# Maxima moved out of the first step of an attention kernel: a lead of 16 visits, two value units and six banks of maxima each

## The chip, the cores and the metric

The kernel runs on one core of a Trainium2 chip. The metric is the device time of one execution in microseconds (us); lower is better. The engines named below are PE (TensorE, matmuls), PEld (its weight loads, which overlap its matmuls), DVE (VectorE), ACT (ScalarE), POOL (GpSimd) and SP (SyncE, here only a queue for DMAs). L341 is line 341 of the kernel before.

## What is computed

Two attentions over the same x (2048 rows, 576 columns, 32 heads of 18), mixed by a gate for each row:

```python
g = _sigmoid((x * gate_w).sum(-1, keepdims=True))
a = _A_ref(x, A_wqkv, A_wo)           # 32 heads, each with its own keys and values
b = _B_ref(x, B_wq, B_wk, B_wv, B_wo) # 32 query heads, one shared key and value head
return g * a + (1 - g) * b
```

Each of the two is softmax(q k / sqrt(18)) v for every head, then a product with wo, in float32. The softmax is taken with the row maximum subtracted.

## The kernel before

**Stages.** The kernel treats the 64 heads alike and calls them u = 0 to 63; the first 32 share one key head. Stage one projects x to queries and keys (project, L147) and writes them to memory in DRAM as a high and a low part. The lead follows: it projects the values (project_v, L187) and computes the first row maxima (step_max, L341 and L350). Then comes the long loop over steps T = 0 to 1023, 16 steps to a head, taken in pairs; then the last output projections.

**A step.** A head has 2048 queries and 2048 keys. For the maxima, step (u, i) takes 128 queries against all keys: four banks of PSUM, each one matmul of 54 rows by 512 columns (pm, L341) and one reduction on DVE (mx, L350). For one step in each pair of the loop there is a shorter way: an extra "x" bank with a difference of keys goes through ACT (xb, L344) and is added by DVE to bank 0 on the fly (L347), so that bank 1 isn't needed. For the scores, step (u, i) takes 128 keys against all queries: four matmuls (ps, L376) and four exponentials on ACT (pt, L383). The values then multiply the exponentials (acc, L390), a step or two behind the scores. The operands lie twice in SBUF, from partition 0 and from partition 64; the argument low of step_max picks the copy at 0. A bank on the one and a bank on the other use different rows of the PE array.

**Maxima run ahead.** The scores of a head need the maxima of all its queries, so the maxima run LEAD = 22 steps ahead of the scores. After the 16 steps of a head, max_rows (L356, L358) reduces the four columns, transposes, splits the result on POOL and sends it by way of DRAM into the two extra rows of the query tile (m_d, then qs).

**The order** is written out by hand: each engine executes in the order in which the loop emits, and an engine waits only where data or a buffer is missing. Strings give the order inside a pair of steps: s a score bank, m and M maxima banks (M from the low copy), A and B the first and second step of the pair, P, h and H the values' matmuls, x the extra bank, V a number of value units.

```python
FIRST = "sA0 mA2 sA1 mA0 sA2 mA3 mA1 sA3 mB0 sB0 mB1 sB1 mB2 sB2 mB3 sB3 x"
PLAIN = "sA0 mA2 sA1 mA0 sA2 mA3 P sA3 mB0 sB0 mB1 sB1 mB2 h sB2 mB3 sB3 x H"
LEADS = "V.A mA0 MA1 mA2 MA3 V.B mB0 MB1 mB2 MB3"
```

The lead is the same loop with T from -22 to -2 and the string LEADS: 11 pairs of steps, so 22 groups of four maxima banks with one or two value units ahead of each, 32 units in all. Step T = 0 uses FIRST: the scores of steps 0 and 1 together with all eight maxima banks of steps 22 and 23. From T = 2 on it is PLAIN.

**Buffers.** Three rings of PSUM banks: ps_s (3 banks, for score banks and for the projections and value units), ps_m (4 banks, for maxima) and ps_o (1, acc). A tile takes the next bank of its ring and waits until the bank's last reader is done: ACT for scores and value units, DVE for maxima. A value unit is 14 matmuls of 288 columns, one copy by ACT into one of three staging tiles (vst, L190) and one DMA from ACT's queue to DRAM (v_d).

**Side work.** Between the steps of the lead, a generator (gates, L272 to L276) takes one step in each pair: it computes the gates with two small ACT operations, one on POOL and one on DVE, and some DMAs from SP. open_ph2 frees the buffers of stage one and opens those of the loop.

Of the kernel before, what the change touches and what calls it, by code (L numbers as in the profile page):

```python
# [8 lines left out]
F32 = mybir.dt.float32  # L9
# [12 lines left out]
NU = 2 * H  # L22
# [5 lines left out]
LEAD = 22  # L28
# [14 lines left out]
def gated_mix_kernel(ctx: ExitStack, tc: tile.TileContext, xT, wall, wv, wo, out):  # L43
    nc = tc.nc
    P = 128

    def dma(o, i, eng=None):
        o, i = (x.bitcast(F32) if x.dtype == F32R else x for x in (o, i))
        return (eng or nc.sync).dma_start(o, i)  # L49
# [3 lines left out]
    ps_s = ctx.enter_context(tc.tile_pool(name="ps_s", bufs=3, space=PSUM))  # L53
    ps_m = ctx.enter_context(tc.tile_pool(name="ps_m", bufs=4, space=PSUM))
# [57 lines left out]
    def split(src, h, l, eng_h, eng_l):  # L112
        if eng_h is nc.scalar:
            nc.scalar.activation(h, src, AF.Copy)
        else:
            eng_h.tensor_copy(h, src)  # L116
        if l is not None:
            eng_l.tensor_tensor(l, src, h.bitcast(F32), op=OP.subtract)
# [65 lines left out]
    def project_v(st_, hf, w):  # L184
        fp = ps_s.tile([P, 512], F32, name="ps")
        for n, (a, b, k, kr) in enumerate(PROJ):
            nc.tensor.matmul(fp[:, 0:288], X[b][:kr, k, st_ * P:(st_ + 1) * P], w[a][:kr, k, :],  # L187
                             start=(n == 0), stop=(n == len(PROJ) - 1))
        t = vst[st_ % 3]
        nc.scalar.activation(t[:, :, 0:18], fp[:, 0:288].rearrange("p (h d) -> p h d", d=18), AF.Copy)  # L190
        dma(v_d[st_, :, 304 * hf:304 * hf + 304], t.rearrange("p h d -> p (h d)"), nc.scalar)
# [5 lines left out]
    WV = []  # L197
# [70 lines left out]
    def gates():  # L268
        z = small.tile([P, 16], F32, name="z")
        dma(z, z_d.rearrange("(p f) -> p f", p=P))  # L270
        yield
        nc.scalar.activation(g2[:, 0, :], z, AF.Exp, scale=1.0)  # L272
        nc.scalar.activation(g2[:, 1, :], z, AF.Exp, scale=-1.0)
        nc.gpsimd.tensor_scalar(g2, g2, 1.0, None, op0=OP.add)
        yield
        nc.vector.reciprocal(g2, g2)  # L276
        yield
        for i in range(2):
            dma(g_d[i].rearrange("(p f) -> p f", p=P), g2[:, i, :])
        yield  # L280
        for i in range(2):
            dma(gu_d[H * i:H * i + H, :], g_d[i:i + 1, :].to_broadcast([H, S]))
# [15 lines left out]
    def open_ph2():  # L298
        ph1.close()
        L["pt"] = ctx.enter_context(tc.tile_pool(name="ppool", bufs=12, side="left"))  # L300
        L["work"] = ctx.enter_context(tc.tile_pool(name="work", bufs=2, side="left"))
        p2 = ctx.enter_context(tc.tile_pool(name="p2", bufs=1, side="right"))
        L["pool"] = p2
        L["ks"] = [p2.tile([P, S], F32R, name=f"ksa{i}") for i in range(2)] + [ksb]
        L["kds"] = [p2.tile([P, 512], F32R, name="kda"), kdb]
        L["oacc"] = p2.tile([P, 16, D], F32, name="oacc")
        for t in L["ks"][:2]:
            for b in (SB, MB):
                dma(t[b + 54:b + 56, :], ones_r)
# [8 lines left out]
    def kst(u):  # L318
        return ksb if u < H else L["ks"][(u - H) % 3]
# [6 lines left out]

    MX = {}

    def step_max(u, i, c, low=False):

        if u not in MX:
            MX[u] = mxs[u] if u < 2 else mxs[2 + u % 3]
        b = SB if low else MB
        if c == "x":
            k = L["kd", u if u >= H else 0][b:b + 54, :]
        else:
            k = kst(u)[b:b + 54, c * 512:(c + 1) * 512]
        pm = ps_m.tile([P, 512], F32, name="pm")  # L340
        nc.tensor.matmul(pm, qs[u % 3][b:b + 54, i * P:(i + 1) * P], k, start=True, stop=True)  # L341
        if c == "x":
            MX["x", u, i] = lead.tile([P, 512], F32, name="xb", bufs=2)
            nc.scalar.activation(MX["x", u, i], pm, AF.Relu)  # L344
        elif c == 0 and ("x", u, i) in MX:
            junk = lead.tile([P, 512], BF16, name="junk", bufs=1)
            nc.vector.tensor_tensor_reduce(junk, pm, MX.pop(("x", u, i)), 1.0, -3e38, op0=OP.add, op1=OP.max,  # L347
                                           accum_out=MX[u][:, i, c:c + 1])
        else:
            nc.vector.tensor_reduce(MX[u][:, i, c:c + 1], pm, axis=AX.X, op=OP.max)  # L350

    def max_rows(u):


        m = ms[u % 2]
        nc.vector.tensor_reduce(m[:, 0:16], MX.pop(u), axis=AX.X, op=OP.max, negate=True)  # L356
        mt = lead.tile([P, 32], F32, name="mt")
        nc.vector.transpose(mt, m)  # L358
        mh = lead.tile([P, 2, 32], F32R, name="mh")
        split(mt, mh[:, 0, :], mh[:, 1, :], nc.gpsimd, nc.gpsimd)  # L360
        md = m_d[u % 4]
        dma(md, mh.rearrange("p a f -> p (a f)"))
        for b in (SB, MB) if u > NU - 3 else (SB,):
            for a in range(2):
                dma(qs[u % 3][b + 54 + a:b + 55 + a, :].rearrange("o (i b f) -> o i b f", b=4, f=32),
                    md.rearrange("(b i) (o a f) -> o a i b f", i=32, o=1, a=2)[:, a, 0:16])
# [19 lines left out]
    def step_pv(u, i, a, b):  # L386


        for j in range(4):
            nc.tensor.matmul(acc[32 * j:32 * j + 19, a:b], v_of(u, i), PT[u, i, j][:, a:b],  # L390
                             start=(i == 0), stop=(i == 15), skip_group_check=True)
        if b == 512:
            for j in range(4):
                del PT[u, i, j]
# [170 lines left out]
    NSTEP = 16 * NU  # L565
    todo = []

    def pull(n):
        while n > 0 and todo:
            try:  # L570
                next(todo[0])
                n -= 1
            except StopIteration:
                todo.pop(0)
# [19 lines left out]
    slow = [gates()]  # L594
# [9 lines left out]
    def due(T, t0, t1, n):  # L604
        return (n * (T - t0 + 1)) // (t1 - t0) - (n * (T - t0)) // (t1 - t0) if t0 <= T < t1 else 0

    vunits = [(st_, hf) for hf in range(2) for st_ in range(16)]

    FIRST = "sA0 mA2 sA1 mA0 sA2 mA3 mA1 sA3 mB0 sB0 mB1 sB1 mB2 sB2 mB3 sB3 x"
    PLAIN = "sA0 mA2 sA1 mA0 sA2 mA3 P sA3 mB0 sB0 mB1 sB1 mB2 h sB2 mB3 sB3 x H"
    UNIT = "sA0 mA2 sA1 mA0 sA2 mA3 P sA3 mB0 sB0 mB1 sB1 mB2 U sB2 mB3 sB3 x Q"
    ALONE = "sA0 sA1 P U sA2 sA3 U sB0 sB1 h U sB2 sB3 H U"
    LEADS = "V.A mA0 MA1 mA2 MA3 V.B mB0 MB1 mB2 MB3"
    for T in range(-LEAD, NSTEP + 2, 2):
        if T == 0:
            open_ph2()
        for f in at.get(T, []) + at.get(T + 1, []):
            f()  # L620
        M = T + LEAD
        if M >= 16 and M % 16 == 0 and M // 16 - 1 < NU:
            max_rows(M // 16 - 1)
        alone = M >= NSTEP
        units = sum(due(t, Tb, Tc, 32) for t in (T, T + 1) for _, _, _, Tb, Tc in SEG)
        for op in (LEADS if T < 0 else FIRST if T == 0 else ALONE if alone else UNIT if units else PLAIN).split():
            k, second, c = op[0], op[1:2] == "B", op[2:]
            if k == "V":
                while len(vunits) > 32 * (-T - 1 - (c == "B")) // LEAD:
                    project_v(*vunits[0], WV[vunits[0][1]])  # L630
                    vunits.pop(0)
            elif k == "x":
                if M + 2 < NSTEP:
                    step_max(*divmod(M + 2, 16), "x")
            elif k in "mM":
                step_max(*divmod(M + second, 16), int(c), k == "M")
            elif k == "s":
                if T < NSTEP:
                    step_scores(*divmod(T + second, 16), int(c), alone)
            elif k == "U":  # L640
                pull(min(units, 1))
                units -= min(units, 1)
            elif T >= 2:
                step_pv(*divmod(T - (2 if k == "P" else 1), 16), 256 * (k == "H"), 256 if k == "h" else 512)
                if k in "HQ" and T % 16 == 0 and T < NSTEP:
                    head_out(T // 16 - 1)
        pull(units)
        if slow and M % 16:
            for _ in range(2 if T > 1000 else 1):
                if slow:  # L650
                    try:
                        next(slow[0])
                    except StopIteration:
                        slow.pop(0)
# [40 lines left out]
```

## Time and profile before

| | us |
|---|---|
| median of 3 runs | 2796.87 |
| lowest and highest | 2795.1, 2798.84 |
| the profiled execution | 2797.98 |
| its span in the profile | 2795.9 |
| PE busy in the span | 2767.0 |
| DVE busy | 2431.6 |
| ACT busy | 2430.6 |

The span is the time from the first to the last recorded instruction; the execution's own time is 2.1 us longer. Busy times are sums over an engine's instructions. A matmul's end is modelled, so PE looks busy while it in fact waits in line; the idle time of PEld, with what ended it, tells more about waits. The lead lies from 207.1 to 286.4 us of the span, the first step of the loop behind it. In rows of the timeline the columns are start, length, engine, line, operation, written and read tile, count, and in brackets the idle time ahead of it with what ended it.

### The profile page before, as it was taken

The page shows a single profiled execution, that of the slowest core. Times are in us where ns is not written, and L with a number is a line of the kernel's source. Part 1 is how long each engine was busy: PE and PEld are TensorE (multiplying, and loading weights), DVE is VectorE, ACT ScalarE, POOL GpSimd, SP SyncE. Part 2 cuts the span into 40 slices and gives each one's busy share as a digit, 9 for nine tenths or more (in the row PEclk, how much of TensorE's full clock was granted, in tenths as well). Part 3 has the DMA queues.
Part 4 walks back from the last instruction along what each step waited for, and adds up shares of the span by engine and source line. Part 5 has one row for each costly group of instructions (what it writes and reads, how often), then busy time and mean ns, then how long its engine had stood idle before and what let it go on. Part 6 is the DMA issues. An engine that isn't in the chain of part 4 may idle for free.

```text
span 2795.9 us, 57640 instructions
## 1 busy us (share of the span) xinstructions
PE 2767.0 (99%) x22140; PEld 1229.2 (44%) x22140; DVE 2431.6 (87%) x4524; ACT 2430.6 (87%) x4768; POOL 207.2 (7%) x364
## 2 busy tenths in 40 slices
PE   7999999999999999999999999999999999999999
PEld 5888433333333333333333444444444443334544
DVE  3346999999999999999999999899898999998865
ACT  3231899999999999999999999999999999998775
POOL 2220000001001000100110001000100011001000
PEclk9999999999999999999999999999999999999999
DMA  8662011111112111211143223232232323233412
GB/s 258 221 230 76 27 33 33 31 47 51 40 26 57 55 32 32 64 47 26 45 101 106 70 74 104 61 85 76 80 84 76 79 71 84 63 95 107 103 36 92
DMA packets 137143, 215.09 MB, mean 77 GB/s; under 512 B 55437, under 2 KB 94301, under 8 KB 125182
## 3 DMA queue, kind: packets, MB, share of 16 engines
q1 hardware_dynamic: 116156, 168.13, 22.6%
q10 hardware_dynamic: 14120, 22.30, 2.2%
q0 software_dynamic: 6592, 20.99, 2.2%
q8 instruction: 174, 2.85, 0.4%
q14 instruction: 101, 0.83, 0.1%
HBM read 137.31 MB, written 64.77 MB: 72 GB/s over the span
## 4 chain that ended last, share of the span: by engine, by line
PE 94%; DMA 3%; DVE 2%; issue 0%; SPq 0%; ACT 0%; POOL 0%; DVEq 0%; ACTq 0%; POOLq 0%
PE ps L376 40%; PE acc L390 38%; PE ps L147 5%; PE pm L341 5%; PE pm L506 4%; PE ps L187 2%; DVE mx L350 1%; DMA xs<-xT 1%; DVE oacc L560 0%; DMA qkl<-pl 0%; SPq L49 0%; DMA ksb<-qkl 0%; DMA qs<-qkh 0%; DMA ksa<-qkh 0%; DVE oacc L514 0%
## 5 line engine op out<-in xcount | busy, mean ns | idle before, releaser
L383 ACT ACTIVATE pt<-ps 128x512 f32<-128x512 f32 x4052 | 2128.6, 612 | 108.2 <-PE pm L341 45.6
L350 DVE TENSOR_REDUCE mx<-pm 128x1 f32<-128x512 f32 x3096 | 1975.9, 683 | 168.0 <-PE pm L341 126.7
L376 PE MATMUL ps<-qs,ksb 56*128 56x512 f32 x2688 | 908.2, 437 | 0.0
L341 PE MATMUL pm<-ksb,qs 54*128 54x512 f32 x2364 | 825.5, 446 | 1.1 <-DVE mx L350 0.3
L376 PEld LDWEIGHTS ps<-qs,ksb 56*128 56x128 f32 x2688 | 437.0, 184 | 685.2 <-ACT pt L383 665.1
L390 PE MATMUL acc<-pt,vb 128*19 128x256 f32 (+1 forms) x6144 | 592.5, 457 | 0.1
L390 PE MATMUL acc<-pt,vg 128*19 128x256 f32 (+1 forms) x5656 | 579.3, 481 | 0.7 <-DVE oe L400 0.4
L376 PE MATMUL ps<-qs,ksa 56*128 56x512 f32 x1364 | 455.7, 437 | 0.0
L341 PE MATMUL pm<-ksa,qs 54*128 54x512 f32 x1232 | 433.5, 443 | 0.0
L341 PEld LDWEIGHTS pm<-ksb,qs 54*128 54x128 f32 x2364 | 379.5, 184 | 10.6 <-DVE mx L350 4.1
L376 PEld LDWEIGHTS ps<-qs,ksa 56*128 56x128 f32 x1364 | 218.2, 184 | 342.9 <-ACT pt L383 316.8
L347 DVE CUSTOM_DVE_ANT_0 junk<-pm,xb 128x512 bf16<-128x512 f32 x500 | 339.9, 680 | 0.0
L344 ACT ACTIVATE xb<-pm 128x512 f32<-128x512 f32 x500 | 305.1, 610 | 0.0
L341 PEld LDWEIGHTS pm<-ksa,qs 54*128 54x128 f32 x1232 | 200.3, 184 | 0.9
L390 PEld LDWEIGHTS acc<-pt,vb 128*19 128x19 f32 x6144 | 104.2, 97 | 209.9 <-issue 199.9
L390 PEld LDWEIGHTS acc<-pt,vg 128*19 128x19 f32 x5656 | 95.9, 97 | 209.0 <-issue 197.7
L341 PE MATMUL pm<-kdb,qs 54*128 54x512 f32 x372 | 148.6, 400 | 0.0
L116 POOL CAST mh<-mt 128x32 fp32r<-128x32 f32 x64 | 13.4, 209 | 1683.4 <-DVE mt L358 1683.4
L156 DVE TENSOR_TENSOR pl<-ps,ph 128x512 fp32r<-128x512 f32 x56 | 38.4, 690 | 98.1 <-ACT ph L150 70.2
L150 ACT ACTIVATE ph<-ps 128x512 fp32r<-128x512 f32 x56 | 33.4, 597 | 102.4 <-PE ps L147 87.4
L147 PE MATMUL ps<-xh,wh 128*128 128x512 f32 x280 | 75.6, 401 | 20.9 <-ACT xh L210 13.4
L147 PE MATMUL ps<-xh,wl 128*128 128x512 f32 x280 | 73.5, 393 | 0.0
(99 smaller groups left out, 1334.7 us busy)
## 6 DMA issues: line engine op xcount, KB each, us to landing
qs<-qkh SPq DMA_DIRECT2D x244, 144.0 KB
qs<-qkl SPq DMA_DIRECT2D x122, 144.0 KB
qkh<-ph ACTq DMA_DIRECT2D x56, 256.0 KB
qkl<-pl POOLq DMA_DIRECT2D x56, 256.0 KB, 3.1
ksa<-qkh SPq DMA_DIRECT2D x88, 144.0 KB
onh<-oh SPq DMA_DIRECT2D x32, 256.0 KB
onl<-ol SPq DMA_DIRECT2D x32, 256.0 KB
oih<-onh SPq DMA_DIRECT2D x16, 512.0 KB
```

The lines of the kernel that those rows point to most:

```text
L147: nc.tensor.matmul(fp, w[a][:kr, k, :], X[b][:kr, k, cs], start=(n == 0), stop=(n == len(PROJ) - 1))
L150: nc.scalar.activation(h, fp, AF.Copy)
L156: nc.vector.tensor_tensor(l, fp, h.bitcast(F32), op=OP.subtract)
L187: nc.tensor.matmul(fp[:, 0:288], X[b][:kr, k, st_ * P:(st_ + 1) * P], w[a][:kr, k, :], start=(n == 0), stop=(n == len(PROJ) - 1))
L341: nc.tensor.matmul(pm, qs[u % 3][b:b + 54, i * P:(i + 1) * P], k, start=True, stop=True)
L344: nc.scalar.activation(MX["x", u, i], pm, AF.Relu)
L347: nc.vector.tensor_tensor_reduce(junk, pm, MX.pop(("x", u, i)), 1.0, -3e38, op0=OP.add, op1=OP.max, accum_out=MX[u][:, i, c:c + 1])
L350: nc.vector.tensor_reduce(MX[u][:, i, c:c + 1], pm, axis=AX.X, op=OP.max)
L376: nc.tensor.matmul(ps, kst(u)[b:b + 56, i * P:(i + 1) * P], qs[u % 3][b:b + 56, c * 512:(c + 1) * 512], start=True, stop=True)
L383: nc.scalar.activation(pt, ps, AF.Exp, scale=SCALE)
L390: nc.tensor.matmul(acc[32 * j:32 * j + 19, a:b], v_of(u, i), PT[u, i, j][:, a:b], start=(i == 0), stop=(i == 15), skip_group_check=True)
L506: nc.tensor.matmul(fp[:, 0:288], o[b][:r, t, s2 * P:(s2 + 1) * P], w[a][:r, t, 288 * hf:288 * hf + 288], start=(n == 0), stop=(n == 3 * nt ...
```

## The change

The lead becomes a loop of its own with 16 visits. Each visit emits two value units, then six maxima banks; 16 x 6 = 96 banks are the steps 0 to 23, two steps more than before. Odd banks use the low copy, as before. Of the six banks, the first two take their PSUM bank from the ring of the scores (ps_s), the other four from ps_m. max_rows of head 0 is emitted at the start of visit 11; before, it was emitted at T = -6, with three of the eleven pairs left. The gate generator takes its steps from visit 4 on. open_ph2 comes after the loop, as before right ahead of T = 0. FIRST, the string of step T = 0, keeps the scores and the x bank and loses its eight maxima banks. The steps from T = 2 on, LEAD and all buffers stay as they are.

```diff
--- before.py
+++ after.py
@@ -326,7 +326,7 @@
     MX = {}
-    def step_max(u, i, c, low=False):
+    def step_max(u, i, c, low=False, pool=ps_m):
@@ -337,7 +337,7 @@
             k = L["kd", u if u >= H else 0][b:b + 54, :]
         else:
             k = kst(u)[b:b + 54, c * 512:(c + 1) * 512]
-        pm = ps_m.tile([P, 512], F32, name="pm")
+        pm = pool.tile([P, 512], F32, name="pm" if pool is ps_m else "ps")
         nc.tensor.matmul(pm, qs[u % 3][b:b + 54, i * P:(i + 1) * P], k, start=True, stop=True)
         if c == "x":
             MX["x", u, i] = lead.tile([P, 512], F32, name="xb", bufs=2)
@@ -604,36 +604,45 @@
     def due(T, t0, t1, n):
         return (n * (T - t0 + 1)) // (t1 - t0) - (n * (T - t0)) // (t1 - t0) if t0 <= T < t1 else 0
     vunits = [(st_, hf) for hf in range(2) for st_ in range(16)]
-    FIRST = "sA0 mA2 sA1 mA0 sA2 mA3 mA1 sA3 mB0 sB0 mB1 sB1 mB2 sB2 mB3 sB3 x"
+    banks = [(M, c) for M in range(LEAD + 2) for c in range(4)]
+    for v in range(16):
+        if v == 11:
+            max_rows(0)
+        for st_, hf in vunits[2 * v:2 * v + 2]:
+            project_v(st_, hf, WV[hf])
+        for n, (M, c) in enumerate(banks[6 * v:6 * v + 6]):
+            step_max(*divmod(M, 16), c, c % 2 == 1, ps_s if n < 2 else ps_m)
+        if v >= 4 and slow:
+            try:
+                next(slow[0])
+            except StopIteration:
+                slow.pop(0)
+    open_ph2()
+    FIRST = "sA0 sA1 sA2 sA3 sB0 sB1 sB2 sB3 x"
     PLAIN = "sA0 mA2 sA1 mA0 sA2 mA3 P sA3 mB0 sB0 mB1 sB1 mB2 h sB2 mB3 sB3 x H"
     UNIT = "sA0 mA2 sA1 mA0 sA2 mA3 P sA3 mB0 sB0 mB1 sB1 mB2 U sB2 mB3 sB3 x Q"
     ALONE = "sA0 sA1 P U sA2 sA3 U sB0 sB1 h U sB2 sB3 H U"
-    LEADS = "V.A mA0 MA1 mA2 MA3 V.B mB0 MB1 mB2 MB3"
-    for T in range(-LEAD, NSTEP + 2, 2):
-        if T == 0:
-            open_ph2()
+    for T in range(0, NSTEP + 2, 2):
         for f in at.get(T, []) + at.get(T + 1, []):
             f()
         M = T + LEAD
-        if M >= 16 and M % 16 == 0 and M // 16 - 1 < NU:
+        if M % 16 == 0 and M // 16 - 1 < NU:
             max_rows(M // 16 - 1)
         alone = M >= NSTEP
         units = sum(due(t, Tb, Tc, 32) for t in (T, T + 1) for _, _, _, Tb, Tc in SEG)
-        for op in (LEADS if T < 0 else FIRST if T == 0 else ALONE if alone else UNIT if units else PLAIN).split():
+        for op in (FIRST if T == 0 else ALONE if alone else UNIT if units else PLAIN).split():
             k, second, c = op[0], op[1:2] == "B", op[2:]
-            if k == "V":
-                while len(vunits) > 32 * (-T - 1 - (c == "B")) // LEAD:
-                    project_v(*vunits[0], WV[vunits[0][1]])
-                    vunits.pop(0)
-            elif k == "x":
+            if k == "x":
                 if M + 2 < NSTEP:
                     step_max(*divmod(M + 2, 16), "x")
-            elif k in "mM":
-                step_max(*divmod(M + second, 16), int(c), k == "M")
+            elif k == "m":
+                step_max(*divmod(M + second, 16), int(c))
             elif k == "s":
                 if T < NSTEP:
                     step_scores(*divmod(T + second, 16), int(c), alone)
```

## The prediction

> **What bounds the kernel now.** I read the page's totals and its chain of work first, then the stages by windows, then the timeline of the two stages that the change touches.
>
> ```profile
> PE 2767.0 (99%) x22140; PEld 1229.2 (44%) x22140; DVE 2431.6 (87%) x4524; ACT 2430.6 (87%) x4768; POOL 207.2 (7%) x364
> ...
> PE 94%; DMA 3%; DVE 2%; issue 0%; SPq 0%; ACT 0%; POOL 0%; DVEq 0%; ACTq 0%; POOLq 0%
> ```
> ```profile
> 285.99:302.00 16.01, 14.93 (x76) 5.54 (x75) 13.37 (x25) 11.56 (x22) 0.00 (x0) 0.79 0.05 15
> 302.00:600.00 298.00, 297.99 (x2578) 113.08 (x2574) 286.14 (x539) 292.09 (x579) 3.69 (x16) 1.00 0.12 31
> ```
> The columns of the windows are length, busy time of PE, PEld, DVE, ACT and POOL, granted clock, DMA share. PE looks full everywhere, but its ends are modelled. In the long loop ACT is busy for 292.09 of 298.00 us, so the loop runs at ACT's pace. The 16 us before it are the odd ones out: ACT at 11.56, clock 0.79. The diff touches only the lead ahead of that stretch and its first step, so I treat everything behind it as shifted.
>
> The lead, from the chain in order of time and from the timeline:
>
> ```profile
> 219.31 2.06 PE ps L187 x14
> 221.37 0.78 PE pm L341 x3
> 222.15 3.88 PE ps L187 x28
> 226.04 0.66 PE pm L341 x2
> ```
> ```profile
> 207.10 0.81 PEld L187 LDWEIGHTS ps<-vwh,xh 128*128 128x128 f32 x5
> ...
> 222.08 0.69 PEld L187 LDWEIGHTS ps<-vwh,xh 128*128 128x128 f32 x5 [0.25 <-ACT vst L190]
> ...
> 225.97 0.73 PE L341 MATMUL pm<-ksb,qs 54*128 54x512 f32 x4
> 226.07 0.41 ACT L190 ACTIVATE vst<-ps 128x288 f32<-128x288 f32 x1 [1.43 <-PE ps L187]
> 226.51 2.48 DVE L350 TENSOR_REDUCE mx<-pm 128x1 f32<-128x512 f32 x4 [2.19 <-PE pm L341]
> ```
> PE sets the pace: two value units back to back take 3.88, four banks after them 0.66; a single unit takes 2.06, and the four banks after it 0.78, because DVE is still draining the previous four (2.48, 0.62 a bank). DVE then waits 2.19.
>
> The first step:
>
> ```profile
> 285.99 0.44 PEld L341 LDWEIGHTS pm<-ksb,qs 54*128 54x128 f32 x4 [0.17 <-issue]
> 286.36 0.19 PEld L376 LDWEIGHTS ps<-qs,ksb 56*128 56x128 f32 x1
> 286.53 7.86 DVE L350 TENSOR_REDUCE mx<-pm 128x1 f32<-128x512 f32 x13 [0.33 <-PE pm L341]
> 287.01 0.60 ACT L383 ACTIVATE pt<-ps 128x512 f32<-128x512 f32 x1 [0.50 <-PE ps L376]
> 287.27 0.18 PEld L341 LDWEIGHTS pm<-ksb,qs 54*128 54x128 f32 x1 [0.73 <-DVE mx L350]
> 287.27 0.50 PE L341 MATMUL pm<-ksb,qs 54*128 54x512 f32 x1 [0.30 <-DVE mx L350]
> 287.85 1.19 ACT L383 ACTIVATE pt<-ps 128x512 f32<-128x512 f32 x2 [0.24 <-PE pm L341]
> 287.87 0.18 PEld L341 LDWEIGHTS pm<-ksb,qs 54*128 54x128 f32 x1 [0.41 <-DVE mx L350]
> 292.88 0.60 ACT L344 ACTIVATE xb<-pm 128x512 f32<-128x512 f32 x1
> 294.68 1.91 PE L390 MATMUL acc<-pt,vb 128*19 128x512 f32 x8
> 296.52 0.28 PEld L376 LDWEIGHTS ps<-qs,ksb 56*128 56x128 f32 x1 [1.68 <-issue]
> 297.35 1.57 ACT L383 ACTIVATE pt<-ps 128x512 f32<-128x512 f32 x3 [2.36 <-PE pm L341]
> 300.26 0.60 ACT L344 ACTIVATE xb<-pm 128x512 f32<-128x512 f32 x1
> 301.35 1.05 PE L390 MATMUL acc<-pt,vb 128*19 128x512 f32 x8
> ```
> DVE bounds it: 13 reductions without a gap, and every score stands on PE behind a bank that waits for DVE (0.73, then 0.41, every 0.60 us). Then the values' matmuls of the second pair run at half speed, 1.91 against 1.05, and ACT idles 2.36.
>
> Where the loop has settled:
>
> ```profile
> 305.31 0.61 ACT L344 ACTIVATE xb<-pm 128x512 f32<-128x512 f32 x1
> 305.78 4.27 ACT L383 ACTIVATE pt<-ps 128x512 f32<-128x512 f32 x8
> 309.94 0.61 ACT L344 ACTIVATE xb<-pm 128x512 f32<-128x512 f32 x1
> ```
> Nine ACT operations from one x bank to the next, 309.94 - 305.31 = 4.63, or 0.514 each. My clock for the whole change is therefore when the x bank of the third pair (T = 4) reaches ACT: 305.31 now.
>
> **The change, part by part.** *The lead.* Before, it runs from 207.10 to the first score's weights at 286.36: 79.26 us for 32 value units and 88 banks in 22 groups. After, 16 visits hold the same units and 96 banks. A visit is 3.88 for the pair plus six banks. Two pairs of banks take 0.73 in their matmul row, one matmul 0.50 (the 287.27 row), so a further pair adds 0.23; if nothing overlapped it would be half of 0.66, 0.33, and at nothing the visit would be 0.23 less. I take 0.23: six banks 0.89, a visit 4.77, 16 visits 76.3. The last group is cut short as now: its score starts 0.37 after the group, not 0.66, so 0.3 less. The first score comes at 207.10 + 76.0 = 283.1, **3.2 us earlier** (between 1.6, with 0.33, and 6.9, with the third pair free). Eight more banks cost less than six group changes and the waits on DVE.
>
> What hides the rest: a visit's six reductions are 6 x 0.62 = 3.72 on DVE, under 4.77. The two banks in the scores' ring of three: a value unit's slot was last held by the second unit of the visit before (or, for the second unit, by its first bank). That unit's eviction ends at 226.48, 4.40 after its pair began at 222.08; the next pair starts at 4.77. So 0.37 us of cover; without it each visit is late by what is missing.
>
> *Moved steps.* Maxima of head 0 go out after visit 10, their DVE work at about 207.10 + 10 x 4.77 + 8.1 = 262.9.
>
> ```profile
> 268.72 0.22 DVE L356 TENSOR_REDUCE m<-mx 128x16 f32<-128x64 f32 x1
> ```
> ```profile
> 272.40 1.23 SPq L49 DMA_DIRECT2D qs<-m_d  x2
> ```
> From there to the end of the last DMA's issue is now 273.63 - 268.72 = 4.9; then 267.8, 15 us ahead of the first score at 283.1 (12.7 now). The gate steps run in visits 4 to 8, in ACT's idle 1.4 us; their DMAs stay on SP ahead of those of the maxima, three visits apart, and nothing else is on SP there. At nothing. The unit 16 uses the staging tile that unit 15 has just filled:
>
> ```profile
> 246.84 0.33 ACTq L49 DMA_DIRECT2D v_d<-vst  x1
> 249.12 0.41 ACT L190 ACTIVATE vst<-ps 128x288 f32<-128x288 f32 x1 [2.31 <-PE ps L187]
> ```
> That is 2.28 us now, with the wait on PE and not on the DMA; after, about 2.5. At nothing.
>
> *The first step.* Eight scores, an x bank, and no maxima, so ACT's 0.514 bounds it where DVE's 0.60 did. The first exponential follows its score by 287.01 - 286.36 = 0.65: 283.75. The second and third scores wait for slots of the last visit's two banks on DVE: 0.74 and 1.34 after DVE's start, as in the rows at 287.27 and 287.87, some 0.2 late in all. The x bank of the first step reaches ACT at 283.95 + 8 x 0.514 = 288.1 (now 292.88), that of the third pair, undisturbed, 9.26 later at 297.3: **8.0 us earlier** than 305.31.
>
> *The clock.* What may be late next is the array's clock:
>
> ```profile
> 286.40:291.50 5.10, 4.11 (x20) 1.49 (x17) 4.97 (x9) 3.75 (x8) 0.00 (x0) 1.00 0.13 43
> 291.50:291.56 0.06, 0.06 (x2) 0.06 (x2) 0.06 (x1) 0.06 (x1) 0.00 (x0) 0.94 0.00 0
> ...
> 291.60:298.35 6.75, 6.67 (x27) 2.31 (x31) 5.03 (x10) 4.13 (x9) 0.00 (x0) 0.50 0.01 2
> 298.45:302.00 3.55, 3.55 (x34) 1.23 (x26) 2.96 (x7) 3.18 (x7) 0.00 (x0) 1.00 0.00 0
> ```
> It fell at 291.55, 5.2 us after the dense lead ended, and came back at 298.37, 3.7 after dense work began again at 294.68. The new first step gives PE nine matmuls in 4.6 us, thinner than the 20 in 5.1. With the same delays: fall at 288.3, the values' matmuls of the second pair at about 288.9, return at 292.6. Then those matmuls take 1.84 (294.68 to 296.52), the next score reaches ACT 0.83 later (296.52 to 297.35), at 291.6, while ACT ran dry at 288.1 + 4 x 0.514 = 290.2: 1.4 lost, and about 0.3 more in the group behind. Bounds: nothing lost if the clock stays, and 300.26 - 292.88 - 4.63 = 2.75 if the second pair is as disturbed as now. I take 1.7, since the dense work follows sooner.
>
> **The sum**: -8.0 + 1.7 = **-6.3 us**. The profiled execution took 2797.98 (span 2795.9, 2.1 around it): 2791.7. It lies 1.1 above the median of the runs shown, 2796.87, so against the median: **2790.6**.
>
> [...]
>
> **The rivals.**
> *The clock stays whole.* PE has a score every 0.514 us in the new step, never idle for long, and the thin stretch is 5.2 us, not 8.3. Against: the fall at 291.55 under more matmuls. No loss: -8.0, 2788.9. [...]
> *The gain is smaller.* Two full stretches of half clock (-8.0 + 2.75 = -5.3), or banks at 0.33 a pair (another 1.6): -3.7 to -5.3, 2791.6 to 2793.2. For it: the rows at 221.37 show that banks do pay for a late drain.
> *The end does not move.* The loop later catches on something timed by DMA and the lead's gain is absorbed: 2796.9. Against: the DMA share is 0.12 in the loop, and PE is 94% of the chain.
> *Slower.* The shared ring: if a visit's first value unit had to wait for its last shared bank on DVE instead of the eviction on ACT, it would start at 3.88 + 0.54 (DVE's start after its bank, 286.53 - 285.99) + 1.24 + 0.1 = 5.76 instead of 4.77. 15 visits x 0.99 = 14.8 lost, -6.3 + 14.8 = +8.5: 2805.4. It decides from 0.42 us a visit (6.3 / 15) for no gain. Against: by the order of allocation the slot is the second unit's.
>
> **How the numbers follow.** Chances: the forecast 0.40, clock whole 0.25, smaller gain 0.20, no move 0.05, slower 0.10. The three runs lie 3.7 us apart, so 0.2%, 5.6 us, is about what can be told from no change; the line is at 2791.3, and the forecast stands only 0.7 clear of it. Faster: three quarters of the forecast 0.30, nearly all of the whole clock 0.24, a little of the smaller gain 0.02: 0.56. Slower 0.10. Same 0.34. Range 2788.0 to 2795.5: it reaches from the whole clock past the smaller gain, and leaves out the slower case, most of no move, and the tail below.
>
> **What the profile after would show.** Visits of 4.77 on PE, banks of six, and no wait of L187 on DVE; the first score near 283; ACT's first eight exponentials 0.52 apart with DVE idle; a stretch of half clock beginning near 288 and shorter than 6.8; the x bank of the third pair near 299; a loop of 4.63 a pair as before. I am wrong if visits are over 5.2, if the half clock lasts longer, or if the loop settles at another pace: 13 ns a pair over 500 pairs would eat the gain.

## The result, and the profile after

| | before | after |
|---|---|---|
| median of 19 runs each, us | 2797.21 | 2791.39 |
| lowest and highest | 2795.1, 2799.5 | 2787.61, 2795.2 |
| the profiled execution (its span) | 2797.98 (2795.9) | 2793.2 (2791.1) |

The ratio of after to before is 0.9978 (95% interval 0.9972 to 0.9984): 0.22% faster, 5.8 us between the medians; 6.3 were forecast (2790.6 for the median of the kernel after). Four fifths of that, 4.8, lie between the two profiled executions.

The page of the kernel after, totals and chain:

```profile
PE 2765.4 (99%) x22140; PEld 1231.9 (44%) x22140; DVE 2431.6 (87%) x4524; ACT 2430.2 (87%) x4768; POOL 207.2 (7%) x364
...
PE 95%; DMA 2%; DVE 1%; SPq 0%; issue 0%; ACT 0%; POOL 0%; DVEq 0%; ACTq 0%; POOLq 0%
```

Nothing to be read there: a change of 5 us in 2800 doesn't show in totals. It shows in the timeline of the kernel after, with the columns as before. Two visits of the lead:

```profile
207.15 0.81 PEld L187 LDWEIGHTS ps<-vwh,xh 128*128 128x128 f32 x5
...
212.05 0.69 PEld L187 LDWEIGHTS ps<-vwh,xh 128*128 128x128 f32 x5 [0.37 <-ACT vst L190]
...
215.96 0.49 PE L341 MATMUL ps<-ksb,qs 54*128 54x512 f32 x2
216.06 0.42 PEld L341 LDWEIGHTS pm<-ksb,qs 54*128 54x128 f32 x4
...
216.49 1.29 DVE L350 TENSOR_REDUCE mx<-ps 128x1 f32<-128x512 f32 x2 [1.04 <-PE ps L341]
...
216.85 0.69 PEld L187 LDWEIGHTS ps<-vwh,xh 128*128 128x128 f32 x5 [0.36 <-ACT vst L190]
...
217.69 2.47 DVE L350 TENSOR_REDUCE mx<-pm 128x1 f32<-128x512 f32 x4
```

A visit takes 216.85 - 212.05 = 4.80: the pair of value units 3.91, the six banks 0.89. DVE idles 1.04 us ahead of the six reductions. Then the first step and the two pairs of steps behind it:

```profile
283.63 0.18 PEld L376 LDWEIGHTS ps<-qs,ksb 56*128 56x128 f32 x1
...
284.30 4.22 ACT L383 ACTIVATE pt<-ps 128x512 f32<-128x512 f32 x8 [0.71 <-PE ps L376]
284.34 0.18 PEld L376 LDWEIGHTS ps<-qs,ksb 56*128 56x128 f32 x1 [0.52 <-DVE mx L350]
...
288.35 0.66 ACT L344 ACTIVATE xb<-pm 128x512 f32<-128x512 f32 x1
...
289.30 1.91 PE L390 MATMUL acc<-pt,vb 128*19 128x512 f32 x8
...
291.97 1.57 ACT L383 ACTIVATE pt<-ps 128x512 f32<-128x512 f32 x3 [1.49 <-PE pm L341]
...
295.51 0.61 ACT L344 ACTIVATE xb<-pm 128x512 f32<-128x512 f32 x1
...
300.26 0.62 ACT L344 ACTIVATE xb<-pm 128x512 f32<-128x512 f32 x1
```

The eight exponentials now run as one row of 4.22 us, where before they came in pieces behind DVE. But the values' matmuls of the second pair still take 1.91, and ACT still idles. The clock, in the windows of the kernel after (length, busy time of five engines, granted clock, DMA share):

```profile
283.63:288.00 4.37, 4.09 (x15) 1.58 (x11) 3.64 (x6) 3.70 (x8) 0.00 (x0) 1.00 0.15 51
288.10:294.80 6.70, 6.70 (x30) 2.20 (x30) 4.11 (x8) 4.21 (x9) 0.00 (x0) 0.50 0.01 4
294.95:298.00 3.05, 3.05 (x28) 1.15 (x28) 2.33 (x6) 2.80 (x7) 0.00 (x0) 1.00 0.00 0
```

A granted clock of 0.50 again for about 6.8 us. What differs is therefore this (us; "first pair" runs from the first score's weights to its x bank on ACT, the next two from x bank to x bank):

| kernel | lead | first pair | second pair | third pair | sum | half clock |
|---|---|---|---|---|---|---|
| before | 79.26 | 6.52 | 7.38 | 5.05 | 98.2 | 6.8 |
| after | 76.48 | 4.72 | 7.16 | 4.75 | 93.1 | 6.8 |

The sum is 5.1 less. What lies ahead of the lead is equal by chance (the first value unit at 207.10 and 207.15), and what lies behind is equal: 2490.6 us from the third pair's x bank to the end before, 2490.8 after.

### The profile page after: what moved, and what is told of

It is laid out like the page before. It is cut to its first block, busy times and chain, and to the rows that moved or that the text cites. A ratio compares the mean times of both kernels' runs of the same rounds, so it can differ in the third digit from the quotient of the medians.

```text
span 2791.1 us, 57642 instructions
## 1 busy us (share of the span) xinstructions
PE 2765.4 (99%) x22140; PEld 1231.9 (44%) x22140; DVE 2431.6 (87%) x4524; ACT 2430.2 (87%) x4768; POOL 207.2 (7%) x364
## 4 chain that ended last, share of the span: by engine, by line
PE 95%; DMA 2%; DVE 1%; SPq 0%; issue 0%; ACT 0%; POOL 0%; DVEq 0%; ACTq 0%; POOLq 0%
PE ps L376 41%; PE acc L390 38%; PE ps L147 5%; PE pm L341 4%; PE pm L506 4%; PE ps L187 2%; SPq L49 0%; DVE oacc L560 0%; DMA ksb<-qkh 0%; DMA xs<-xT 0%; DVE mx L350 0%; DMA qs<-qkl 0%; DVE oacc L514 0%; DMA vg<-v_d 0%; PE pm L376 0%
## 5 line engine op out<-in xcount | busy, mean ns | idle before, releaser
L341 PE MATMUL pm<-ksb,qs 54*128 54x512 f32 x2332 | 814.4, 444 | 0.0
```

## The experiments

Total times scatter by 4 to 8 us within one kernel, as much as the effect, so the stages of the traces carry the verdicts, one trace for each run, and the times come beside them. For all kernels the rest behind the third pair took 2490.5 to 2491.2 us: every difference is ahead of it, in the columns of this table or in the start of the first value unit (last column).

| run | lead | first pair | second pair | third pair | sum | half clock | first unit at |
|---|---|---|---|---|---|---|---|
| e11, before again | 79.27 | 6.53 | 7.29 | 5.03 | 98.1 | 6.8 | 203.46 |
| e8, after again | 76.49 | 4.71 | 6.14 | 4.62 | 92.0 | 3.4 | 206.16 |
| e12, after, third trace | 76.49 | 4.71 | 5.62 | 4.63 | 91.5 | 3.4 | 207.29 |
| e1, lead only | 76.40 | 7.52 | 6.96 | 5.03 | 95.9 | 6.8 | 205.42 |
| e2, step only | 80.77 | 4.59 | 6.84 | 4.61 | 96.8 | 6.8 | 204.63 |
| e3, one ring | 99.17 | 4.59 | 5.92 | 4.63 | 114.3 | 6.8 | 201.39 |
| e4, late slots | 88.16 | 6.14 | 5.72 | 4.63 | 104.7 | 3.4 | 203.68 |
| e5, fillers, waiting | 76.49 | 7.09 | 6.25 | 4.61 | 94.4 | 6.8 | 206.49 |
| e6, fillers before | 79.26 | 6.86 | 5.04 | 4.62 | 95.8 | none | 207.78 |
| e7, half the fillers | 76.49 | 6.97 | 5.55 | 4.64 | 93.7 | 6.8 | 202.99 |
| e9, fillers | 76.48 | 4.72 | 4.68 | 4.61 | 90.5 | none | 205.86 |
| e10, fewer fillers | 76.49 | 4.71 | 4.67 | 4.62 | 90.5 | none | 207.44 |

### The lead alone, and the first step alone

*e1_lead_only*: the new lead with the 88 banks of before.

```diff
-    banks = [(M, c) for M in range(LEAD + 2) for c in range(4)]
+    banks = [(M, c) for M in range(LEAD) for c in range(4)]
-        if v == 11:
+        if v == 12:
-        for n, (M, c) in enumerate(banks[6 * v:6 * v + 6]):
+        for n, (M, c) in enumerate(banks[11 * v // 2:11 * (v + 1) // 2]):
-    FIRST = "sA0 sA1 sA2 sA3 sB0 sB1 sB2 sB3 x"
+    FIRST = "sA0 mA2 sA1 mA0 sA2 mA3 mA1 sA3 mB0 sB0 mB1 sB1 mB2 sB2 mB3 sB3 x"
```

> The lead in 16 visits, but with the 88 banks of before (five and six in turn), and the first step with its eight maxima banks as before. Theory (the gain comes from the regrouping of the lead): the first score comes at 282.8 to 283.6 us of the span instead of 286.36, the first step stays at DVE's pace (6.5 us from the first score to the x bank on ACT), and the x bank of the third pair comes 2.8 to 3.6 earlier than 305.31; total 2.8 to 3.6 under the kernel before. Rival (the gain comes from taking the maxima out of the first step): the x bank of the third pair comes less than 1 us earlier.

The lead got shorter by 2.86 as expected, but the first pair took 7.52 instead of 6.5. DVE's rows in e1 say why:

```profile
281.78 1.29 DVE L350 TENSOR_REDUCE mx<-ps 128x1 f32<-128x512 f32 x2 [1.71 <-PE ps L341]
282.99 7.86 DVE L350 TENSOR_REDUCE mx<-pm 128x1 f32<-128x512 f32 x13
```

The last group has six banks instead of four, two more reductions ahead of those of the first step, and DVE paces that step. 2.3 us were left in the sum, between theory and rival; the median of 2793.93 (before 2796.84) and the ratio, 0.9997 (0.9988 to 1.0006), can't tell it from no change.

*e2_step_only*: the new first step, the lead in 24 groups of four.

```diff
-    for v in range(16):
-        if v == 11:
+    for v in range(24):
+        if v == 17:
             max_rows(0)
-        for st_, hf in vunits[2 * v:2 * v + 2]:
-            project_v(st_, hf, WV[hf])
-        for n, (M, c) in enumerate(banks[6 * v:6 * v + 6]):
-            step_max(*divmod(M, 16), c, c % 2 == 1, ps_s if n < 2 else ps_m)
+        while len(vunits) > 32 * (23 - v) // 24:
+            project_v(*vunits[0], WV[vunits[0][1]])
+            vunits.pop(0)
+        for M, c in banks[4 * v:4 * v + 4]:
+            step_max(*divmod(M, 16), c, c % 2 == 1)
```

> The first step without maxima, but the lead in 24 groups of four banks with one or two value units ahead of each, as before in kind. Theory (regrouping): 24 groups cost 8 x 4.54 + 16 x 2.84 - 0.3 = 81.5 us, 2.2 more than before, and the first steps give 2.3 back (18.95 us from the first score to the x bank of the third pair before, 16.63 after): x bank of the third pair at 305.2, total within 0.5 us of the kernel before. Rival (the first step): 2 us or more faster than before.

The lead grew by 1.5, not 2.2, and the pairs gave back 2.9, not 2.3: 1.4 less in the sum; the median 2794.32, the ratio 0.9991 (0.9982 to 1.0000). So neither half makes the whole gain, and the theory that the regrouping makes it alone falls. Eight more banks cost 1.5 in groups of four and 0.1 in groups of six (76.48 against 76.40 in e1, whose groups of five banks take 0.89 us and those of six 0.90): the regrouping pays the price of the move.

### The shared ring

*e3_one_ring*: all six banks in the ring of four.

```diff
-            step_max(*divmod(M, 16), c, c % 2 == 1, ps_s if n < 2 else ps_m)
+            step_max(*divmod(M, 16), c, c % 2 == 1)
```

> The changed kernel with all six banks of a visit in the ring of four. Theory (the two borrowed slots are what lets six banks go out at once): the fifth bank waits for DVE until 1.28 us after the first, the sixth until 1.88, a visit takes 1.4 more, 6.2 instead of 4.79, 16 visits some 22 us more: about 2813 in all. Rival (DVE idles 1.1 us a visit, so slots don't matter): no difference to the changed kernel.

```profile
230.30 0.73 PE L341 MATMUL pm<-ksb,qs 54*128 54x512 f32 x4
...
231.58 0.18 PEld L341 LDWEIGHTS pm<-ksb,qs 54*128 54x128 f32 x1 [0.98 <-DVE mx L350]
...
232.17 0.18 PEld L341 LDWEIGHTS pm<-ksb,qs 54*128 54x128 f32 x1 [0.41 <-DVE mx L350]
232.60 0.70 PEld L187 LDWEIGHTS ps<-vwh,xh 128*128 128x128 f32 x5 [0.24 <-issue]
```

The timeline of e3 has the expected numbers: the fifth bank 1.28 after the first, the sixth 1.87, a lead 22.7 us longer than in the kernel after. (The one time, 2808.61, is lower than the 2813 expected because this execution began its value units at 201.39.) DVE idles 2.5 us in each visit, and yet PE waits for it. Without the two borrowed slots the change is slower than the kernel before, 114.3 against 98.2 in the sum.

*e4_late_slots*: the borrowed slots for the last two banks.

```diff
-            step_max(*divmod(M, 16), c, c % 2 == 1, ps_s if n < 2 else ps_m)
+            step_max(*divmod(M, 16), c, c % 2 == 1, ps_s if n > 3 else ps_m)
```

> The changed kernel with the two borrowed slots given to the last two banks of a visit instead of the first two. Theory (the cover is the order of DVE's work: a second value unit takes the slot of the first borrowed bank): that slot is free only after the fifth reduction, the second unit starts 1.0 us late, a visit takes 5.8 instead of 4.79, 15.5 us in all, and the second and third score of the first step wait some 2 us more: 2807 to 2810 in all, and PE's weight loads of L187 wait for DVE. Rival (slots are free in time anyway): no difference.

```profile
230.92 0.70 PEld L187 LDWEIGHTS ps<-vwh,xh 128*128 128x128 f32 x5 [0.36 <-ACT vst L190]
...
233.08 0.41 ACT L190 ACTIVATE vst<-ps 128x288 f32<-128x288 f32 x1 [2.52 <-PE ps L187]
...
233.54 0.69 PEld L187 LDWEIGHTS ps<-vwh,xh 128*128 128x128 f32 x5 [0.73 <-ACT vst L190]
...
291.84 0.18 PEld L376 LDWEIGHTS ps<-qs,ksb 56*128 56x128 f32 x1
...
292.50 0.60 ACT L383 ACTIVATE pt<-ps 128x512 f32<-128x512 f32 x1 [0.72 <-PE ps L376]
293.15 0.18 PEld L376 LDWEIGHTS ps<-qs,ksb 56*128 56x128 f32 x1 [1.13 <-ACT pt L383]
```

Slower than the kernel after: the lead by 11.7 us instead of 15.5, the first pair by 1.4, the one time 2800.88 (expected 2807 to 2810; its value units began 3.5 us earlier). But the mechanism isn't the one expected. The second unit starts right after ACT has copied the first out (233.49), 0.78 late in each of 15 visits, and the second score right after the first exponential (293.10). So a tile doesn't take the next bank of its ring in turn, as I had assumed: here it took the one that ACT had just read, rather than one still queued on DVE (the fifth bank's reduction in the last visit began only at 294.20). Where the borrowed slots stand in the visit decides, as expected; which reader is waited for was wrong.

### The half clock

*e5_fill_after* and *e7_half_fill* give PE matmuls that nobody reads in the first step, to see whether its thin work lets the clock fall. Nothing of the computation is left out.

```diff
+    def filler():
+        if "f" not in L:
+            L["f"] = ps_m.tile([P, 512], F32, name="pm")
+        nc.tensor.matmul(L["f"], qs[1][SB:SB + 54, 0:P], ksb[SB:SB + 54, 0:512], start=True, stop=True)
...
-    FIRST = "sA0 sA1 sA2 sA3 sB0 sB1 sB2 sB3 x"
+    FIRST = "sA0 d sA1 d sA2 d sA3 d sB0 d sB1 d sB2 d sB3 d x"
```

> The changed kernel with one more matmul behind each of the eight scores of the first step, of 54 rows by 512 columns on the same rows of the array, into a bank that nobody reads: work for PE alone, nothing for DVE or ACT. Theory (the half clock after the first step comes from PE's thin work there, and costs 2.5 us: 7.16 from the x bank of the first to that of the second pair, where the loop takes 4.63): the clock stays whole, the second pair takes 4.6 to 5.0, the values' matmuls 1.05 instead of 1.91; 2.2 to 2.6 us faster than the changed kernel. Rival (the clock falls for another reason, or the fillers delay the scores as much as the clock gives back): the second pair still takes 7 us, or the first step grows by 1 us or more; no gain.

> [...]

The string of e7 has a filler behind every second score alone: "sA0 d sA1 sA2 d sA3 sB0 d sB1 sB2 d sB3 x".

```profile
283.21 0.40 PE L381 MATMUL ps<-qs,ksb 56*128 56x512 f32 x1
...
284.88 0.18 PEld L371 LDWEIGHTS pm<-ksb,qs 54*128 54x128 f32 x1 [1.72 <-DVE mx L350]
...
287.21 0.63 PE L381 MATMUL ps<-qs,ksb 56*128 56x512 f32 x1
```

Neither filled the step, and e5's timeline shows why: the first filler (L371) took a bank that DVE still had to read, so the weight loads stood still for 1.72 us in the very step that was to be filled (1.71 in e7). The first pair grew by 2.4, and the clock fell at 286.9. They show only this: with PE idle for 1.28 us ahead of the first filler (284.88), and with a matmul each 0.24 us on average from 285.22 on, it still fell. e7's time was 2789.51, one run with an early start (202.99), which says nothing; e5's ratio is 0.9987 (0.9979 to 0.9996).

*e6_fill_before*: the fillers of e5 in the first step of the kernel before, `"sA0 d mA2 sA1 d mA0 sA2 d mA3 mA1 sA3 d mB0 sB0 d mB1 sB1 d mB2 sB2 d mB3 sB3 d x"`.

> The kernel before with the same eight fillers in its first step. Theory: the clock stays whole here too, the second pair takes 4.6 to 5.2 instead of 7.38, the first step stays at DVE's pace (6.5 from the first score to the x bank): 2.2 to 2.7 us faster than before. That would leave some 3 us of the change's gain to the lead and to ACT's pace in the first step. Rival: no difference.

Windows of e6, then two rows of its timeline:

```profile
286.90:294.00 7.10, 6.57 (x34) 3.19 (x32) 6.77 (x12) 5.15 (x10) 0.00 (x0) 1.00 0.11 33
294.00:299.00 5.00, 4.92 (x42) 1.90 (x41) 4.77 (x9) 4.47 (x10) 0.00 (x0) 1.00 0.01 2
```
```profile
294.98 1.05 PE L395 MATMUL acc<-pt,vb 128*19 128x512 f32 x8
295.96 0.50 PE L381 MATMUL ps<-qs,ksb 56*128 56x512 f32 x1
```

The clock stays whole, the values' matmuls take 1.05, the second pair 5.04 instead of 7.38; the first pair grew by 0.3, which was not expected, and the sum is 2.4 less. The times don't show it: ratio 0.9997 (0.9988 to 1.0005), an interval that holds both -2.4 us and nothing.

*e9_fill_both* and *e10_fill_low* mend e5: the filler writes to acc, which nothing uses until the second pair and which the values' first matmuls overwrite.

```diff
+    def filler(b):
+        if b == MB and "f" not in L:
+            L["f"] = ps_m.tile([P, 512], F32, name="pm")
+        nc.tensor.matmul(L["f"] if b == MB else acc, qs[1][b:b + 54, 0:P], ksb[b:b + 54, 0:512], start=True, stop=True)
...
-    FIRST = "sA0 sA1 sA2 sA3 sB0 sB1 sB2 sB3 x"
+    FIRST = "sA0 e sA1 e sA2 e sA3 d e sB0 d e sB1 d e sB2 d e sB3 d e x"
```

In e10 the d are left out and every score is followed by e alone (d works on the rows from partition 64, e on those from 0).

> The changed kernel with a matmul of 54 rows behind each score of the first step, into the bank acc, which nothing else uses yet (no slot to wait for), and from the fourth score on a second one on the other rows of the array, into one bank of the maxima's ring, which is free by then. [...] Theory (PE's thin work makes the clock fall; the fillers of e5 and e7 failed because the first filler waited 1.7 us for a slot that DVE still read, and so left PE idle): the first step stays at 4.7 us from the first score to the x bank, the clock stays whole, the second pair takes 4.6 to 5.0 instead of 6.1 to 7.2: the x bank of the third pair comes 90.2 to 90.8 us after the first value unit (93.1 and 92.0 in the two looks at the changed kernel, 98.2 before). Rival (the clock falls whatever PE does there): 92 to 93.

> [...] If what counts is the time in which PE works, the clock stays whole as in e9 (90.2 to 90.8). If it is how much of the array works, it falls as in the changed kernel, and the fillers, twice as long at half clock, hold up the scores besides: 92 to 95.

The timeline of e9, the pair behind the first step:

```profile
282.34 0.18 PEld L381 LDWEIGHTS ps<-qs,ksb 56*128 56x128 f32 x1
...
287.06 0.66 ACT L344 ACTIVATE xb<-pm 128x512 f32<-128x512 f32 x1
...
287.53 4.32 ACT L388 ACTIVATE pt<-ps 128x512 f32<-128x512 f32 x8
287.70 0.14 PEld L395 LDWEIGHTS acc<-pt,vb 128*19 128x19 f32 x8 [0.24 <-issue]
287.70 1.05 PE L395 MATMUL acc<-pt,vb 128*19 128x512 f32 x8
...
291.74 0.61 ACT L344 ACTIVATE xb<-pm 128x512 f32<-128x512 f32 x1
```

Eight exponentials without a gap in the second pair, 4.68 from x bank to x bank, the whole clock, 90.5 in the sum: both kernels come near the prediction's rival "the clock stays whole" (8.0 under before; 98.2 - 90.5 = 7.7). It was thin work, then: of the fourteen traces the eleven in which the first step left PE thin fell to a granted clock of 0.50, for 3.4 or 6.8 us, and the three in which fillers kept it at work (e6, e9, e10) stayed at 1.00. e10 kept the clock on the scores' own 54 rows, as the reading by time would have it; but it doesn't settle that reading. Counted as 54 of the 128 rows that a value unit's matmul uses (128*128 in its rows), e10 stands at 40% (two matmuls of 0.23 in 0.49, times 0.42), and the pairs of the kernel before, which fell, at 32% (two in 0.60): by this count, too, the step that fell has less work than the one that did not. Both beat the kernel before: e9 2788.80 against 2796.64, ratio 0.9970 (0.9959 to 0.9981); e10 2789.96, 0.9973 (0.9963 to 0.9983). That they beat the changed kernel is shown by the traces (1.0 to 2.6 us), not by the times, whose intervals overlap with its own.

*e8_after_again*, *e11_before_again*, *e12_after_third*: the two kernels unedited, to see what repeats.

> [...]

> [...]

> [...]

e8 gave 2790.96, ratio 0.9978 (0.9968 to 0.9988); e11 and e12 one run each (2794.65 and 2792.05). Windows of e8:

```profile
282.65:287.60 4.95, 4.66 (x19) 1.79 (x15) 4.06 (x7) 4.29 (x9) 0.00 (x0) 1.00 0.14 45
287.70:291.00 3.30, 3.30 (x14) 1.08 (x16) 1.49 (x5) 1.85 (x5) 0.00 (x0) 0.50 0.03 7
291.10:295.00 3.90, 3.90 (x38) 1.19 (x34) 3.58 (x8) 3.89 (x9) 0.00 (x0) 1.00 0.00 0
```

Half clock for 3.4 us here, as in e12, and for 6.8 in the first trace of the changed kernel; in the kernel before 6.8 both times. e11's sum is 98.1 where the first trace of the kernel before has 98.2. Lead and first pair repeat to 0.01 us. The half clock came in one or two lengths of 3.41 us. From the last change of clock in stage one to the fall it is 62 such lengths in the kernel after (76.42 to 288.04) and 63 in the one before (76.51 to 291.55). Against the first x bank the fall came 0.31 us ahead, 0.31 behind and 0.95 ahead in the three traces of the changed kernel, with two, one and one lengths at 0.50. So the fall has no fixed place in the kernel; what sets its place, and what decides between one length and two, isn't shown. PE was not without work ahead of these falls: it began a matmul at least every 0.60 us up to them (from 283.86 to 288.04 in the kernel after, from 287.27 to 291.55 in the one before).

## Why the prediction was right

**The lead.** Forecast 16 visits of 4.77 and the first score 3.2 us earlier; measured 4.79 (76.48 for all) and 2.8. The first visit took 4.90 us (207.15 to 212.05) and the others 0.02 to 0.03 more than forecast; the last group gave back 0.3, as forecast. That six banks go out in 0.89 was right, and DVE drains them while the next units run, as forecast; e3 shows the price when there are not banks for all six. The moved steps cost nothing, as forecast: no visit from the second to the fifteenth differs from 4.79 or 4.80 us, and the issue of the last DMA of head 0's maxima ended at 267.70, where 267.8 was forecast, 16 us ahead of the first score.

**The first step.** ACT's pace instead of DVE's: 288.1 forecast for its x bank, 288.35 measured, with the second score waiting for DVE as forecast. Over all traces of the two kernels the change gained 2.8 in the lead and 1.8 here; 1.0 in the second and 0.4 in the third pair make up the 6.0 between the mean sums.

**The clock.** Taken at 1.7 us lost in the second pair, between 0 and 2.75. Measured against the loop's 4.63: 2.5, 1.5 and 1.0 in the three traces, 1.7 in the mean. The first of them came near the worst case, so its sum is 5.1 and not 6.3 under that of before; the other two are 6.2 and 6.8 under 98.2. In that trace the half clock was not shorter than 6.8, as the prediction said that it would be, and the x bank of the third pair came at 300.26 instead of near 299. That 1.7 is the mean is luck: it came from delays that the traces don't bear out. My delay ("3.7 after dense work begins") did not hold: the half clock lasted 6.8 us in the first trace and 3.4 in the other two, and it began between 0.95 us ahead of the first x bank and 0.31 behind it.

**The rest is shifted.** 2490.6 against 2490.8 behind the third pair; the loop settles at 4.62 (300.26 to the next x bank below), as before.

```profile
304.88 0.61 ACT L344 ACTIVATE xb<-pm 128x512 f32<-128x512 f32 x1
```

**The rivals.** "The clock stays whole" happened in no trace of the changed kernel, but in e9 and e10 near its price. "The gain is smaller" by as much half clock as before was the profiled execution (-5.3 forecast, -5.1 measured): its "two full stretches" are the two lengths of 3.41 us that make the 6.8 in both kernels' first traces. "Slower" by the shared ring didn't come: in the kernel after each visit's first unit waits for ACT, 0.36 us, and none for DVE. Its price was right in kind (e4: 11.7 us in the lead by slots badly placed), but my rule for which bank a tile takes was wrong. The forecast stood only 0.7 us clear of the 0.2% that the prediction took as what can be told from no change; the interval of the ratio, 0.16 to 0.28%, lies on both sides of it.

## What to carry to other kernels

Group work on PE by what its reader drains meanwhile: the same 96 banks took a lead of 76.48 us in groups of six behind two units and 80.77 in groups of four (e2), but only with banks for all six (e3: 99.17); and it matters which of the six borrow a bank (e4: 88.16). The first step, in which PE began one matmul each 0.49 us, also cost 1.0 to 2.5 us behind its end, at a granted clock of 0.50: eight matmuls for nobody, into a bank that is free, won that back in the trace (e10: second pair 4.67, clock 1.00). And where runs scatter by more than the effect, find a point from which all traces are equal and compare what lies ahead of it.

## What the runs showed that I had not expected

**How much work is thin.** By the time in which PE works, one matmul of 0.23 us (the spacing in e9's fillers) each 0.49 (47%, after) or a pair at once each 0.60 (38%, before) went with a granted clock of 0.50 behind them, and so did 1.28 us without work and then a matmul each 0.24 us (e5); with two, one after the other, in 0.60 (77%, e6) or in 0.49 (e10) it stayed at 1.00. Whether the time or the rows at work make the difference stays open (e10).

**The start scatters.** The first value unit, behind the same code, came between 201.39 and 207.78 us. The chain in order of time of the kernel before and of e3 shows where they part:

```profile
63.95 6.88 DMA qkl<-pl
70.93 0.70 DVE pl L156
71.67 135.36 PE ps L147 x586
```
```profile
39.86 6.38 DMA wst<-wall
46.31 0.33 ACTq L49
46.69 0.74 ACT wh L126
47.48 154.30 PE ps L147 x672
```

On the chain PE gets free of its waits for DMAs at 71.67 in the one and at 47.48 in the other. Between the two profiled executions of the kernel before, the start accounts for the whole difference in time (3.64 us earlier, 3.33 less). That it also makes most of the 4 to 8 us between the executions without a trace is not shown, and what orders those DMAs wasn't tried.
